# The last wait of a decode kernel, moved from SyncE's program to GpSimd's

## The chip, the cores and the metric

The kernel runs on one core of a Trainium2 chip. A core has five engines that each run a program of their own: TensorE (PE in the profile, its weight loads PEld), VectorE (DVE), ScalarE (ACT), GpSimd (POOL) and SyncE (SP). They meet only through semaphores: an instruction or a transfer adds to one, another instruction waits until it has a given value. SyncE computes nothing; here it issues nearly all transfers between the chip's main memory (HBM) and the on-chip buffer.

The metric is the device time of one execution in microseconds (us), as a median of several. It covers more than the instructions of the kernel: the span, from the first to the last recorded instruction of the program, is a little shorter than the measured time.

## The reference

One decode step for two sequences (one new token each, 512 features): attention over a cached context of 4096 positions with 32 heads of 128, a small two-layer network on the same two tokens, and a gate that mixes the two results.

```python
g = sigmoid((A_x * gate_w).sum(-1))
q = A_x @ A_wq                                      # 2 x (32 heads x 128)
p = softmax(q . A_k_cache * 128 ** -0.5)            # over 4096 positions, per head
a = (p . A_v_cache) @ A_wo                          # 4096 -> 512
b = relu(A_x @ B_w1) @ B_w2                         # 512 -> 1376 -> 512
out = g * a + (1 - g) * b                           # 2 x 512, bfloat16
```

Both halves read A_x. Keys and values are 64 MB each, so the 145 MB that are read set the scale of the work.

## The kernel before

The keys and the values (2 sequences x 32 heads x 4096 rows of 128) are cut into 8 units each, 32768 rows or 8 heads a unit. Three regions of the on-chip buffer take the units in turn, in the order written out in `order` (L185): five units of keys, then values and keys alternating, then the rest of the values. SyncE issues each unit's transfer as soon as TensorE is done with the unit that last used its region. VectorE transposes the keys, TensorE makes scores, ScalarE the exponentials, GpSimd spreads the probabilities into a masked layout, and TensorE multiplies them with the values. The last unit of values comes in two transfers (LASTV, L20).

After the last unit SyncE issues w2 (L252) and the output weights wo in four pieces (L255, WO_IN at L231), each with a semaphore of its own, wo0 to wo3. In the end TensorE runs `project` (L615): 32 steps of two products, each pair accumulating 2 x 512 results, the later steps waiting for the pieces of wo. When the last product is done, VectorE (L623) and ScalarE (L625) each convert one half of the result to bfloat16 and add 1 to the semaphore `cast`. SyncE waits for `cast` to be 2 and issues the output's transfer (L257), 2 KB, which adds 16 to the semaphore `out` when it has landed. Then SyncE waits for `out` to be 16 (L258, added by the call at L694).

All of this is written out by hand. Each helper (`sp`, `pool`, `dve`, `act`, `pe`) appends an operation to the list of one engine in `_Prog`; at the end `emit` (L77) writes the lists, each engine's operations in the order in which they were appended. An operation's waits become separate conditions ahead of it. So the order of calls at the bottom of the function is the order of each engine's program; only the relative order of calls for the same engine matters.

Three of the programs have operations in their ends that compute nothing: `fill` (L609) appends n increments of a semaphore that nobody waits for (L613). ScalarE gets five after its last copy ahead of the final half (L688) and five after it (L695), VectorE three and five (L689, L696), GpSimd three at once (L690) and four more that wait for the third piece of wo (L691). GpSimd's last real work is the spreading of the probabilities for the last unit of values; after that its program holds only these increments. TensorE's program ends with a branch that is never taken back (`never_back`, L634). Nothing in the kernel follows SyncE's wait for the output.

The lines around the change:

```python
    sp(lambda e: e.dma_start(out.rearrange("b s n -> (b s) n"), out_sb).then_inc(sem["out"], 16), dwaits=[(sem["cast"], 2)])
    tail_sp = [lambda: sp(lambda e: e.wait_ge(sem["out"], 16))]
...
    fill("pool", 3)
    fill("pool", 4, [(sem["wo2"], 16)])
    project()
    never_back()
    tail_sp[0]()
    fill("act", 5, [(sem["cast"], 2)])
    fill("dve", 5, [(sem["cast"], 2)])
```

Of the kernel before, what the change touches and what calls it, by code (L numbers as in the profile page):

```python
# [94 lines left out]
def bass_gated_mix__gqa_block_cached__dense_activation_relu__decode_kernel(  # L95
# [12 lines left out]
    P = _Prog(nc)  # L108
# [71 lines left out]
    sem = {n: nc.alloc_semaphore("sem_" + n) for n in names}  # L180
# [20 lines left out]
    def sp(fn, waits=(), dwaits=()):  # L201
        P.add("sp", fn, waits=waits, dwaits=dwaits)
# [52 lines left out]
        sp(lambda e, i=i, a=a, b=b: e.dma_start(wo_sb[:, a * 512:b * 512], A_wo.rearrange("(p r) n -> p (r n)", r=32)[:, a * 512:b * 512])  # L255
           .then_inc(sem[f"wo{i}"], 16))
    sp(lambda e: e.dma_start(out.rearrange("b s n -> (b s) n"), out_sb).then_inc(sem["out"], 16), dwaits=[(sem["cast"], 2)])  # L257
    tail_sp = [lambda: sp(lambda e: e.wait_ge(sem["out"], 16))]  # L258


    def constants():
# [347 lines left out]
    def fill(name, n, dwaits=()):  # L609
        if name not in P.fill:  # L610
            P.fill[name] = nc.alloc_semaphore("fill_" + name)
        for i in range(n):
            P.add(name, lambda e: e.sem_inc(P.fill[name], 1), dwaits=(dwaits if i == 0 else ()))  # L613
# [20 lines left out]
    def never_back():  # L634
        def fn(e):
            e.reg_mov(reg["p"], 1)
            e.br_lt(reg["p"], 1, on_true="rest", on_false="last").branch_hint(hint[0])
            enter("last", "main", engines=[mybir.EngineType.PE, mybir.EngineType.DVE, mybir.EngineType.Activation, mybir.EngineType.Pool,
                                   mybir.EngineType.SP])
        pe(fn)  # L640
# [50 lines left out]
    fill("pool", 4, [(sem["wo2"], 16)])  # L691
    project()
    never_back()
    tail_sp[0]()  # L694
    fill("act", 5, [(sem["cast"], 2)])  # L695
    fill("dve", 5, [(sem["cast"], 2)])  # L696

    P.resolve()

# [35 lines left out]
```

## Time and profile before

| | |
|---|---|
| measured time, median of 3 runs | 342.76 us (342.52 to 342.91) |
| the profiled execution: its own time | 342.64 us |
| the profiled execution: its span | 341.3 us |
| mean granted TensorE clock | 0.835 |
| read from HBM | 145.43 MB, 426 GB/s over the span |
| TensorE, VectorE, GpSimd, ScalarE busy | 209.9, 155.4, 41.8, 13.9 us |
| SyncE's issue of the output (L257) | starts at 340.13 us, takes 0.33 |
| SyncE's wait for the output (L258) | ends with the span, at 341.3 us |

A profile is one execution. Times in it count from the start of the span, and instructions are named by engine and by line of the kernel (L257 is line 257). An engine's name with a q (SPq, POOLq) stands for its sequencer, which waits, branches and issues transfers; that time is not counted as busy. A waiting instruction is recorded from the moment at which its wait is over, so its start tells when it was released. The view "chain that ended last" follows work back from the end; it starts at the last instruction that counts as work, so waits and transfers after that are not in it and have to be read from the timeline, from the view of an engine's waits and from single source lines.

Beside instructions, the trace records the time of each change of each semaphore, the landings of transfers included, and each packet that a transfer queue moved. These records go on for about 1.4 us after the last instruction of the kernel, up to 342.76 us.

### The profile page before, as it was taken

The numbers are of one execution on the slowest core, as the hardware profiler recorded it, in microseconds if no ns is written. First come the engines' busy times: TensorE is split into PE (matmuls) and PEld (weight loads), VectorE is DVE, ScalarE is ACT, GpSimd is POOL, SyncE is SP. The second block draws the span as 40 slices with busy tenths as digits, with TensorE's granted clock in tenths as the row PEclk, the third lists the DMA queues.
The fourth block names the chain that finished last, engine by engine and source line by source line (L and its number), as shares of the span: only waits on it lengthen the run. The fifth ranks groups of instructions, "written<-read, shape, count | busy, mean of one in ns | idle before, by whom it ended". The sixth has DMA issues, their size and how long they took to land. (4 is left out here: it accounts for less than half of the span.)

```text
span 341.3 us, 3101 instructions
## 1 busy us (share of the span) xinstructions
PE 209.9 (61%) x1243; PEld 33.9 (10%) x843; DVE 155.4 (46%) x45; ACT 13.9 (4%) x37; POOL 41.8 (12%) x53
## 2 busy tenths in 40 slices
PE   0080079685968909972995059820993773718387
PEld 0040011000100101110111001100100100101024
DVE  1010897979799769229800693019805000000111
ACT  2001000000000020000000000000003000000000
POOL 1000000000000004005002300050000235050400
PEclk9999999999898965996799559965696659676789
DMA  8998989898999999998989898989999999999896
GB/s 346 434 492 369 492 369 492 369 492 369 492 392 468 399 461 445 415 484 376 492 369 492 369 492 369 492 369 492 392 468 392 468 438 424 398 441 461 374 440 264
DMA packets 3580, 145.46 MB, mean 426 GB/s; under 512 B 405, under 2 KB 634, under 8 KB 762
## 3 DMA queue, kind: packets, MB, share of 16 engines
q1 hardware_dynamic: 3460, 145.33, 98.7%
q10 hardware_dynamic: 118, 0.10, 0.1%
q8 instruction: 1, 0.02, 0.0%
q14 instruction: 1, 0.01, 0.0%
HBM read 145.43 MB, written 0.00 MB: 426 GB/s over the span
## 5 line engine op out<-in xcount | busy, mean ns | idle before, releaser
L404 DVE STREAM_TRANSPOSE kv<-kv 128x8192 uint32<-128x8192 uint32 (+1 forms) x17 | 138.6, 8186 | 74.4 <-DMA kv<-in_A_k_cache_dram 74.4
L314 PE MATMUL PS<-kv,zero 128*128 (+1 forms) x544 | 130.3, 421 | 40.4 <-PEq L481 40.4
L314 PE MATMUL PS<-kv,ptw 128*32 x512 | 48.1, 469 | 11.7 <-issue 11.5
L320 PE MATMUL PS<-zero 32*128 32x512 bf16 (+2 forms) x21 | 9.7, 537 | 57.6 <-ACT zero L410 20.3
L449 POOL TENSOR_TENSOR ptw<-E,mask 128x512 bf16<-128x512 bf16 x32 | 32.2, 1038 | 21.1 <-PE PS L314 10.9
L467 DVE TENSOR_TENSOR X<-PS,maskc 128x512 f32<-128x512 f32 x2 | 1.4, 692 | 64.1 <-PE PS L314 64.1
L314 PEld LDWEIGHTS PS<-kv,zero 128*128 (+1 forms) x144 | 13.6, 103 | 154.6 <-issue 154.6
L393 POOL TENSOR_TENSOR zero<-q_sb,mask 128x32 bf16<-128x32 bf16 x8 | 1.9, 251 | 147.0 <-PE PS L314 123.3
L471 POOL TENSOR_TENSOR X<-X,maskc 128x512 f32<-128x512 f32 x6 | 6.2, 1039 | 109.2 <-ACT X L470 109.2
L314 PE MATMUL PS<-X,zero 128*64 128x512 f32 x16 | 11.6, 819 | 12.3 <-PEq L481 12.3
L314 PEld LDWEIGHTS PS<-kv,ptw 128*32 x512 | 8.7, 99 | 50.4 <-issue 49.7
L320 PEld LDWEIGHTS PS<-zero 32*128 32x128 bf16 x21 | 2.1, 109 | 69.4 <-issue 43.7
L373 DVE STREAM_TRANSPOSE ptw<-PS 128x1024 f32<-128x1024 f32 x1 | 1.3, 1251 | 16.4 <-PE PS L320 16.4
L415 DVE TENSOR_REDUCE zero<-PS 128x2 f32<-128x2048 f32 x2 | 4.5, 2271 | 9.1 <-PE PS L314 9.1
L470 ACT ACTIVATE X<-PS 128x512 f32<-128x512 f32 x6 | 3.6, 597 | 71.4 <-PE PS L314 71.4
L422 ACT ACTIVATE nrow<-mmax 128x32 f32<-128x32 f32 x2 | 0.5, 228 | 132.8 <-DVE mmax L419 132.8
L440 DVE STREAM_TRANSPOSE E<-E 128x2048 bf16<-128x2048 bf16 x2 | 4.6, 2300 | 2.4 <-ACT E L430 2.4
L410 ACT ACTIVATE zero<-zero 1x1 f32<-1x1 f32 x9 | 1.8, 200 | 84.9 <-DMA kv<-in_A_v_cache_dram 67.9
L430 ACT ACTIVATE E<-PS,negm 128x1024 bf16<-128x1024 f32 x4 | 4.4, 1109 | 0.6 <-DVE negm L426 0.6
L284 PE MATMUL PS<-kv 3*128 3x3 bf16 x4 | 0.3, 165 | 6.5 <-DMA kv<-in_gate_w_dram 6.5
L598 PE MATMUL PS<-kv,oW 128*2 128x256 bf16 x64 | 4.0, 272 | 0.4 <-DMA kv<-in_A_wo_dram 0.4
L314 PEld LDWEIGHTS PS<-X,zero 128*64 (+1 forms) x16 | 1.8, 161 | 15.8 <-issue 15.6
(49 smaller groups left out, 27.6 us busy)
## 6 DMA issues: line engine op xcount, KB each, us to landing
kv<-in_A_v_cache_dram SPq DMA_DIRECT2D x1, 6144.0 KB, 36.7
kv<-in_A_wq_dram SPq DMA_DIRECT2D x1, 4096.0 KB, 15.0
kv<-in_A_wo_dram SPq DMA_DIRECT2D x1, 2560.0 KB, 35.9
kv<-in_A_v_cache_dram SPq DMA_DIRECT2D x1, 2048.0 KB, 41.3
kv<-in_B_w_dram SPq DMA_DIRECT2D x1, 1376.0 KB, 5.8
kv<-in_B_w_dram SPq DMA_DIRECT2D x1, 1280.0 KB, 30.1
kv<-in_A_wo_dram SPq DMA_DIRECT2D x1, 1024.0 KB, 37.9
kv<-in_A_wo_dram SPq DMA_DIRECT2D x1, 384.0 KB, 38.4
```

The source lines that it names most:

```text
L314: return e.add_instruction(mybir.InstMatmult(name=nc.get_next_instruction_name(), engine=mybir.EngineType.PE, ins=[rhs, lhsT], outs=[e.low ...
L320: return e.matmul(dst, lhsT=nil, rhs=nil.unsqueeze(1).to_broadcast([32, 4, 128]) if n == 512 else nil[:, 0:n], start=not stop, stop=stop, ...
L393: pool(lambda g: g.tensor_tensor(out=out, in0=q, in1=msk, op=ALU.mult), waits=([["act_q", "dve_mask8"], []] + [[f"pesc_{x}"] for x in rang ...
L404: ins = v.transpose(out=reg[:, 4096 * p0:4096 * p1], in_=reg[:, 4096 * p0:4096 * p1])
L410: return lambda a: a.activation(out=tick[:, 2 + i:3 + i], in_=tick[:, 0:1], func=ACT.Copy).then_inc(sem["go"], n)
L415: dve(lambda v: v.tensor_reduce(out=mpad[:, 0:2], in_=PSF[:, 0:2048].rearrange("p (x h q) -> p h x q", h=2, q=16), axis=AX.XY, op=ALU.max) ...
L430: act(lambda a, h=h: a.activation(out=E[:].rearrange("p (x h q) -> p h x q", h=2, q=16)[:, h], in_=PSF[:, 0:2048].rearrange("p (x h q) -> ...
L440: dve(lambda v: v.transpose(out=E[:], in_=E[:]), waits=[f"act_exp{b}"], signal=f"dve_et{b}")
L449: pool(lambda g, src=src, dst=dst: g.tensor_tensor(out=dst, in0=src, in1=msk, op=ALU.mult), waits=(([f"dve_et{b}"] if ub == 0 else []) + ( ...
L470: act(lambda e: e.activation(out=X2[:], in_=src, func=ACT.Copy), waits=[f"pe_v_{v}"], signal=f"act_x_{v}")
L471: pool(lambda e: e.tensor_tensor(out=X, in0=X, in1=msk, op=ALU.mult).then_inc(sem["xg"], 1), waits=[f"act_x_{v}"] + ([] if v else ["dve_se ...
L598: pe(lambda e, g=g: e.matmul(psf(64 * g, 64 * g + 2, FIN_C0, 256), lhsT=w, rhs=m[:, 256 * g:256 * g + 256], start=start, stop=stop, tile_p ...
```

## The change

SyncE's wait for the output is removed, and the same wait is appended to GpSimd's list, after its increments. SyncE's program now ends with the issue of the output (L257). In the built program that is all: each engine has the same instructions in the same order, except that the wait for `out` stands as the last instruction of GpSimd instead of the last of SyncE.

```diff
     sp(lambda e: e.dma_start(out.rearrange("b s n -> (b s) n"), out_sb).then_inc(sem["out"], 16), dwaits=[(sem["cast"], 2)])
-    tail_sp = [lambda: sp(lambda e: e.wait_ge(sem["out"], 16))]
...
     project()
     never_back()
-    tail_sp[0]()
     fill("act", 5, [(sem["cast"], 2)])
     fill("dve", 5, [(sem["cast"], 2)])
+    P.add("pool", lambda e: e.wait_ge(sem["out"], 16))
```

## The prediction, made before the result was known

> **What bounds the kernel, and its end.** I read the page first, then the chain that ended last, then what SyncE waited for, then the timeline of the last microseconds, and at last the times at which semaphores changed. The page gives the span; over it the 16 DMA engines are busy in nearly every slice, so the body is a stream of transfers:
>
> ```profile
> span 341.3 us, 3101 instructions
> ...
> DMA  8998989898999999998989898989999999999896
> ...
> q1 hardware_dynamic: 3460, 145.33, 98.7%
> ```
>
> The change touches nothing of that stream. In the chain (start, duration, what) the stream ends with the last piece of wo, and a short tail follows:
>
> ```profile
> 300.10 37.89 DMA kv<-in_A_wo_dram
> 337.99 0.04 issue
> 338.03 1.64 PE PS L598 x24
> 339.67 0.02 issue
> 339.69 0.41 DVE ptw L623
> ```
>
> The tail goes on outside the chain, since waits and DMA issues are not counted as work. The timeline from 338 has the two casts and the issue of the output, and the view of SyncE's waits (waiter, what ended the wait, total us, times, longest) has the line that the change takes out of SyncE:
>
> ```profile
> 339.69 0.38 ACT L625 ACTIVATE ptw<-PS 2x256 bf16<-2x256 f32 x1 [5.21 <-PE PS L598]
> 339.69 0.41 DVE L623 CAST ptw<-PS 2x256 bf16<-2x256 f32 x1 [5.82 <-PE PS L598]
> 340.13 0.33 SPq L257 DMA_DIRECT2D out_dram<-ptw  x1
> ```
>
> ```profile
> SPq L258 <- DMA out_dram<-ptw: 0.8, 1, 0.8
> ```
>
> The views by source line place the waiting instruction and the increments that fill the ends of the other programs:
>
> ```profile
> L258 SPq EVENT_SEMAPHORE  x1: 17/17/17, 341.3 to 341.3; - x1
> ```
>
> ```profile
> L613 ACTq EVENT_SEMAPHORE  x10: 17/17/17, 334.3 to 340.7; - x10
> L613 DVEq EVENT_SEMAPHORE  x8: 21/21/21, 333.5 to 340.9; - x8
> L613 POOLq EVENT_SEMAPHORE  x7: 17/17/17, 315.8 to 339.6; - x7
> ```
>
> So SyncE's wait ends the span, at 341.329 us. GpSimd's program was over at 339.638, and the output is last in either kernel. What can differ is only what lies between the landing of the output and the end of the measured time: the profiled execution took 342.64 us, 1.31 more than its span. The trace shows that stretch through semaphores. Number 2 is named by no instruction of the kernel and changes nine times just after it, then nine times again (us from the span's start):
>
> ```
> first nine    340.003 340.938 340.976 341.175 341.446 | 341.489 341.527 341.561 341.608
> second nine   342.399 342.433 342.471 342.515 342.538 | 342.637 342.676 342.710 342.756
> ```
>
> I read each nine as a closing round in which five engines take turns up and then down. Steps in which nobody is late are 34, 38, 44 and 23 ns. Answers to ordinary semaphores, from the change waited for to the waiter's own change, cost ScalarE 45 ns (340.114 to 340.159), GpSimd 49 (339.003 to 339.052) and VectorE 57 (340.114 to 340.171): about 11 more than 34, 38 and 44, in the same order. So the second turn is ScalarE's, the third GpSimd's, the fourth VectorE's; the fifth, fastest and latest, is SyncE's, and the first TensorE's. The late turns fit: 340.938 follows ScalarE's last increment (340.722), 341.175 VectorE's (340.931), and 341.446 SyncE's wait (341.312).
>
> **The change, part by part.**
>
> *Removed: one wait at the end of SyncE.* Its program then ends with the issue, at 340.131 + 0.331 = 340.462 us, 0.87 earlier. With SyncE's own 0.134 from its last instruction's start to its turn, it would be ready near 340.6. By itself this uncovers VectorE: the fourth turn stays at 341.175 and the fifth would follow 0.023 later, 0.25 us before today's 341.446. Nothing stands behind the removed wait in SyncE's queue, and no transfer is issued there later.
>
> *Added: one wait at the end of GpSimd.* It is moved past GpSimd's seven increments (L613), which have no readers, and GpSimd issues no transfers; behind the wait stands only the closing round, and for that all five engines wait. The landing itself doesn't move: the casts, the issue and its packets stay as they are, with the last change of the output's semaphore at 341.296. The 0.25 us are thus never seen: GpSimd's turn, the third, now comes last.
>
> *The sum from the landing on.* Before: SyncE's wait starts 0.016 us after the landing and its turn is 0.134 later (341.446); from the fifth turn to the ninth 0.162 (341.608). That is 0.312 us.
> After: (a) GpSimd's answer: its L613 increment that waits for a landing started 0.024 after it (339.003 to 339.027). (b) From the start of its last instruction to its turn: the trace doesn't show it, since GpSimd had been done for long. Near rows: SyncE 0.134, ScalarE 0.216 (340.722 to 340.938), VectorE 0.244 (340.931 to 341.175). I take 0.23, between ScalarE and VectorE, as GpSimd's increments come every 0.08 us against 0.07 and 0.095 for those two. Ends: not below 0.025 (an increment's own time, 339.027 to 339.052); and not above 1.355, since GpSimd's third turn came at 340.976, right behind the second, counted from its last increment at 339.621. (c) From the third turn to the ninth with all others waiting: in the second nine 0.285 (342.471 to 342.756); in a round ahead of the kernel in which the third turn was the late one, 0.301. I take 0.293. It is more than four steps' 0.162 as two turns are added and as VectorE, just past its fourth turn, is not at once ready for its sixth (0.122 between them in the second nine).
> Sum: 0.024 + 0.23 + 0.293 = 0.547 us, against 0.312: **+0.235 us**. With the near rows' ends it is 0.443 to 0.569, so +0.13 to +0.26; with the far ends +0.02 to +1.37. All of these are losses, since the links after the landing grow in number whatever (b) is; a gain would have to come from outside this round (below).
>
> [...]
>
> **How it goes on the clock.** The profiled execution's 342.64 + 0.235 is 342.88 us. It lies 0.12 below the median of the three timed runs, 342.76 (342.52 to 342.91); on the median the change gives 342.995, **343.0 us**. That is +0.07%, inside the 0.2% that is about what a measurement of this kernel can tell from no change.
>
> **Rivals.**
>
> *Slower: GpSimd stalls on its way to the closing round.* There are gaps in the ends of three programs that no wait explains: between the last two increments (L613) of ScalarE from 340.360 to 340.722 (0.36 us), of VectorE from 340.448 to 340.931 (0.48), and in GpSimd from 339.123 to 339.537 (0.41). They stand close to the end of each program, hidden today behind the output. If one more instruction in GpSimd brings such a gap behind the wait, it adds 0.36 to 0.48, and the change costs +0.60 to +0.72; the far end of (b) gives +1.37, 344.1 us on the median. It decides from (b) = 0.69 on: above that the loss is over 0.2%. Against: GpSimd's gap lies before its last two increments, so the added instruction comes after it; and GpSimd idles some 1.7 us in the wait, time enough to have fetched what follows.
> [...]
>
> *Faster: SyncE's closing work sets the end.* After 341.329 the trace has two transfers of the instruction kind on queue 14, at 341.410 (0.53 us) and 341.620 (0.49, to 342.113). If they are SyncE's and the end waits for them, SyncE's earlier end starts them up to 0.87 earlier: 342.76 - 0.87 = 341.9 us, -0.25%. Against: the fifth turn of the second nine comes 0.023 after the fourth, so SyncE was not late there; TensorE, first in it at 342.399, was.
>
> *Nothing: the measured time doesn't hang on the round's end.* If it hung on the landing alone, the time would stay at 342.76. Against: 1.31 us of the measured time lie around the span, while the round's first part after it takes 0.28.
>
> **Chances.** Forecast (+0.02 to +0.55): 0.62. Slower rival (+0.55 to +1.4): 0.20, of which 0.17 beyond +0.69. Faster rival: 0.10, of which 0.08 beyond -0.69. Nothing: 0.08. So faster 0.08, same 0.75, slower 0.17. The range is 342.4 to 344.1 us: below, the lowest timed run less a tenth, as a time that stays may also fall there; above, the far end of (b) on the median. It leaves out the faster rival.
>
> **What would show it.** In the profile of the changed kernel the span should stay at 341.3 us, now ended by GpSimd's wait (start near 341.32, if the landing stays), SyncE's program should end near 340.46, and the time beyond the span should grow from 1.31 to about 1.55. In semaphore 2's first nine, the long pause should lie before the third change, some 0.25 us after the landing, with the last six in a row in about 0.29. A third change 0.7 us or more after the landing would be the slower rival. A time below 342.1, or second nine that do not shift with the first, would break the picture of the round. An output that lands at another distance from its issue (1.165 us now, 340.131 to 341.296) would be a cause I have priced at nothing.

## The result, and the profile after

The changed kernel takes 343.18 us (median of 18 runs, 343.05 to 343.55), the kernel before 342.64 us in its runs on the same chips (18 runs, 342.48 to 343.39). The ratio is 1.0015 with a 95% interval of 1.0008 to 1.0021: a loss of about 0.5 us. The interval lies above 1, so there is a loss, though at 0.15% it is under the 0.2% that the prediction took as what can be told from no change. The prediction had 343.0 us and +0.235 us: the direction and the way are right, but the forecast's size is under half of the +0.54 measured.

The page's span, and the chain from the last piece of wo on (start, duration, what), of the changed kernel:

```profile
span 341.6 us, 3101 instructions
```

```profile
299.43 38.89 DMA kv<-in_A_wo_dram
338.32 0.04 issue
338.37 1.60 PE PS L597 x24
339.97 0.02 issue
339.99 0.41 DVE ptw L622
```

The chain is the one of before, with about the same durations behind wo; all of it lies 0.30 us later. I take that for the spread between executions and not for an effect of the change: this one took 343.48 us, the second longest of the 18 (the 18 runs of the kernel before differ by 0.91 us among themselves), and the casts were over at 340.416 against 340.114 before, ahead of anything that the change touches. So I compare from the landing of the output on. The timeline has the issue of the output as SyncE's last line, the view of SyncE's waits (window from 290 us) has lost its line for the output, and the source line of the added wait shows when it ended:

```profile
340.43 0.33 SPq L257 DMA_DIRECT2D out_dram<-ptw  x1
```

```profile
SPq L257 <- DVE ptw L622: 39.6, 1, 39.6
SPq L252 <- PE PS L313: 13.8, 1, 13.8
```

```profile
L695 POOLq EVENT_SEMAPHORE  x1: 17/17/17, 341.6 to 341.6; - x1
```

The issue starts at 340.432 and the output lands at 341.598, 1.166 us later (1.165 before). GpSimd's wait ends the span, 0.041 us after the landing (0.033 before, by SyncE). What grew lies behind: the measured time is 1.841 us longer than the span in this execution, 1.311 before. It does so in every run: with the spans rounded to 0.1 us, the difference has a median of 1.84 us over 18 runs (1.81 to 1.88), and of 1.29 over 21 runs of the kernel before (1.26 to 1.35).

The changes of semaphore 2, from each kernel's own landing of the output (us):

```
before  first   -1.293 -0.358 -0.320 -0.121 0.150 | 0.193 0.231 0.265 0.312     second from 1.103
after   first   -1.292 -0.359  0.579  0.622 0.645 | 0.743 0.781 0.817 0.864     second from 1.652
```

The pause has moved from before the fifth change to before the third, as it should if the third turn is GpSimd's. The other numbers tell the size: 0.579 from the landing to that turn, where I had 0.254. From the ninth change to the measured end it is 1.03 us before and 1.02 after. "Measured end" stands here and below for the measured time counted from the start of the span. No record shows where the measurement itself begins and ends, and the last change of semaphore 2 comes 0.12 to 0.13 us behind that point; so what the argument rests on is that the distance stays the same, and not how long it is.

### The profile page after: what moved, and what is told of

It is laid out like the page before. It is cut to its first block, busy times and chain, and to the rows that moved or that the text cites. A ratio compares the mean times of both kernels' runs of the same rounds, so it can differ in the third digit from the quotient of the medians.

```text
span 341.6 us, 3101 instructions
## 1 busy us (share of the span) xinstructions
PE 209.6 (61%) x1243; PEld 33.8 (10%) x843; DVE 155.4 (45%) x45; ACT 13.9 (4%) x37; POOL 41.8 (12%) x53
## 5 line engine op out<-in xcount | busy, mean ns | idle before, releaser
L313 PEld LDWEIGHTS PS<-zero,kv 128*128 (+1 forms) x44 | 3.0, 158 | 3.5 <-issue 3.5
```

Of the source, the lines that this page charges most:

```text
L313: return e.add_instruction(mybir.InstMatmult(name=nc.get_next_instruction_name(), engine=mybir.EngineType.PE, ins=[rhs, lhsT], outs=[e.low ...
```

## The experiments

The theory: the measured end follows the ninth change at a fixed distance; the ninth change follows the turn of whichever engine is late; each engine has a stretch of its own between its last instruction and its turn; and GpSimd's is long, 0.555 us, against SyncE's 0.134. The rivals: a gap as in the ends of the programs that the added instruction brought behind the wait; a slow start after a release, whatever the engine; and a gain from SyncE's early end that is hidden under a larger loss. A version without any wait for the output, which would show what is next late, was not tried: its program could end before the output's semaphore had its last change.

**Four increments behind GpSimd's wait.**

```diff
     P.add("pool", lambda e: e.wait_ge(sem["out"], 16))
+    fill("pool", 4)
```

> As the changed kernel, with four more increments in GpSimd's program behind its wait for the output. The three theories of the 0.555 us between the start of that wait and GpSimd's turn in the closing round: (1) a long stretch of GpSimd's own at the end of any program: the increments come 0.08 apart, the last one's start to the turn is again 0.55, the wait's start to the turn 0.87, and the time beyond the span is that of the changed kernel, while the span grows by 0.33. (2) A gap like the 0.41 before GpSimd's last two increments, at a place counted in instructions from the program's start, now just behind the wait: it shows between two of the four increments, and the last one's start to the turn is 0.14 to 0.23. (3) Slow first steps after any release: the gap shows between the wait and the first increment, and the last one's start to the turn is about 0.23.

343.28 us in the profiled execution; the output lands at 341.128. GpSimd's increments by source line, the last of them ending the span at 341.4:

```profile
L612 POOLq EVENT_SEMAPHORE  x11: 17/17/17, 315.7 to 341.4; - x11
```

The wait merged into the first of the four, so they start at 341.152, 341.230, 341.308 and 341.387, without a gap. The third change is at 341.972: 0.585 from the last increment, 0.820 from the first. A gap among the instructions and a slow start after the release are both out; the long stretch lies behind all of the kernel's own instructions. The third change is 0.27 later after the landing than in the changed kernel, and so is the measured end (2.15 against 1.88).

**No increments in GpSimd's program.**

```diff
-    fill("pool", 3)
-    fill("pool", 4, [(sem["wo2"], 16)])
```

> As the changed kernel, without GpSimd's seven increments: its wait for the output follows its last real work directly, and the gap of 0.41 us that stood before the last two increments has no increments to stand between. (1) Long stretch of GpSimd's own: the wait's start to the turn is 0.555, plus 0.41 if the gap is a place in the program and now falls behind the wait, so 0.97, and the measured time is 343.6 us. (2) A gap that the added instruction brought behind the wait: with seven instructions fewer it falls elsewhere, and the stretch is 0.14 to 0.23 or again 0.55. (3) Slow release: 0.55.

343.18 us. The source line of GpSimd's wait:

```profile
L693 POOLq EVENT_SEMAPHORE  x1: 17/17/17, 341.3 to 341.3; - x1
```

The wait starts at 341.325 and the third change is at 341.880: 0.555 again, to the nanosecond. My 0.97 is wrong: the gap of 0.41 us, which in the profiles with these increments stands before the last two of the seven, doesn't show up in front of the turn. So the seven increments have no part in the 0.555.

The semaphore records show where the gap most likely went. Between the two nines most semaphores change once more, in five groups of about fifty numbers each. The group from 105 to 155 begins 0.057 to 0.060 us after the ninth change in the eleven other profiles and 0.414 after it here; the other four groups begin as in those profiles. GpSimd's is the only program that is shorter here, so I take this group for GpSimd's, and the 0.36 us for the gap, which lengthens the step from one increment to the next by about as much (0.431 against 0.079 in the kernel before): it sits at a place counted in GpSimd's instructions, and with seven fewer it lies behind the turn. There it costs nothing, as the second nine begins 0.778 us after the ninth change against 0.783 to 0.791 in the others.

**The wait in ScalarE's program, in VectorE's, in TensorE's.**

```diff
-    P.add("pool", lambda e: e.wait_ge(sem["out"], 16))
+    P.add("act", lambda e: e.wait_ge(sem["out"], 16))
```

and the same with "dve" and "pe".

> The wait for the output stands last in ScalarE's program instead of GpSimd's. Round theory (the end follows the waiting engine's turn, each engine with its own stretch): 0.02 from the landing to the wait, 0.22 to ScalarE's turn, the second, and 0.32 for the seven turns that follow it in an unbroken round: 0.56 from the landing to the ninth change against 0.31 with the wait in SyncE and 0.86 in GpSimd, so about 342.9 us. Rival (a program released by the output is slow to the round whatever the engine): 0.02 + 0.55 + 0.32 = 0.90, 343.2 us.

> The wait for the output stands last in VectorE's program. Round theory: 0.03 from the landing to the wait, 0.24 to VectorE's turn, the fourth, and 0.24 for the five that follow: 0.51 from the landing to the ninth change, about 342.85 us. Rival (slow release whatever the engine): 0.03 + 0.55 + 0.24 = 0.82, 343.15 us.

> The wait for the output stands last in TensorE's program, behind its branch. Round theory: TensorE has the first turn, so all nine follow the landing: 0.03 to the wait, a stretch of TensorE's own that is not known (0.13 as ScalarE's in the wait's form, up to 0.58, what its branch's start to its turn was before), and 0.357 for the unbroken round: 0.52 to 0.97 from the landing to the ninth change, so a measured time of 1.02 more than that after the landing (1.02 is the distance from the ninth change to the measured end in all six profiles so far). If the first turn is not TensorE's, the first change stays before the landing, and a later one moves.

342.63, 342.68 and 343.34 us in the profiled executions, which differ in when the output lands; so again from the landing on. The wait's line in each of the three:

```profile
L695 ACTq EVENT_SEMAPHORE  x1: 17/17/17, 341.1 to 341.1; - x1
```

```profile
L695 DVEq EVENT_SEMAPHORE  x1: 21/21/21, 341.3 to 341.3; - x1
```

```profile
L695 PEldq EVENT_SEMAPHORE  x1: 51/51/51, 341.7 to 341.7; - x1
```

With the two kernels of the study (us; the last column is the measured time less the landing):

```
wait in    landing  to wait  wait to turn  turn    to the ninth  sum    to the measured end
SyncE      341.296  0.016    0.134         fifth   0.162         0.312  1.344
VectorE    341.225  0.027    0.166         fourth  0.242         0.435  1.455
ScalarE    341.125  0.021    0.131         second  0.324         0.476  1.505
TensorE    341.696  0.028    0.238         first   0.359         0.625  1.644
GpSimd     341.598  0.024    0.555         third   0.285         0.864  1.882
```

In each it is the waiting engine's change that follows the landing, and the changes ahead of it stay before the landing. So the order of the turns is TensorE, ScalarE, GpSimd, VectorE, SyncE. The last column less the sum is 1.02 to 1.03 in all five. A slow start whatever the engine is out: ScalarE and VectorE are quicker to their turns than I had them (0.131 and 0.166 where I had 0.22 and 0.24 from their increments). SyncE has the shortest sum of the five.

**VectorE's wait, timed, and both waits.**

```diff
     P.add("pool", lambda e: e.wait_ge(sem["out"], 16))
+    P.add("sp", lambda e: e.wait_ge(sem["out"], 16))
```

> The wait in VectorE's program, timed. Its one profile had 0.435 us from the landing to the ninth change against 0.312 before and 0.864 in the changed kernel; so +0.12 us on the kernel before (342.76 on 342.64), which 0.2% can't tell from no change, and 0.43 less than the changed kernel's 343.18. A rival by which the time follows the number of turns behind the wait alone (six behind GpSimd's turn, five behind VectorE's, four behind SyncE's) has it midway between the two, +0.27.

> Both waits: SyncE's as before and GpSimd's as changed. Round theory: SyncE's turn, the fifth, is behind GpSimd's third, which comes 0.58 after the landing, so SyncE's wait costs nothing: 0.86 from the landing to the ninth change, 343.18 us, +0.15% on the kernel before, as the changed kernel. If removing SyncE's wait had gained something that GpSimd's wait then overspent, the time would be longer than 343.18 by that much.

With the wait in VectorE 342.63 us (11 runs), ratio 1.0004 (0.9995 to 1.0013); the kernel before had 342.55 in these rounds. That can't be told from no change by itself. The measured time less the span, which leaves out when the output lands, has a median of 1.41 us, 0.12 over before's 1.29, as the sums say (0.435 less 0.312); the rival's +0.27 is out. With both waits it is 343.14 us, ratio 1.0017 (1.0008 to 1.0027), and 1.84 beyond the span, as in the changed kernel. SyncE's wait is over at the same time as GpSimd's:

```profile
L695 POOLq EVENT_SEMAPHORE  x1: 17/17/17, 341.1 to 341.1; - x1
```

```profile
SPq L696 <- DMA out_dram<-ptw: 0.8, 1, 0.8
```

The first line is the source line of GpSimd's wait, the second that of SyncE in the view of its waits. From the landing to the ninth change it is 0.863 us against 0.864 in the changed kernel. So SyncE's wait costs nothing beside GpSimd's, and its removal gains nothing: no gain is hidden under the loss.

**A drain behind the wait.**

```diff
     P.add("pool", lambda e: e.wait_ge(sem["out"], 16))
+    P.add("pool", lambda e: e.drain())
+    fill("pool", 2)
```

> As the changed kernel, with a drain and two increments in GpSimd's program behind its wait for the output. What GpSimd does in the 0.555 us of its own is open; one candidate is a drain. If a drain of the idle engine is what takes long, the first increment comes 0.3 to 0.5 us after the wait, and the ones behind the drain start 0.08 apart. If a drain of the idle engine is short, the first increment comes 0.1 to 0.2 after the wait. In both cases the last increment's start to the turn is again 0.585, as with four increments, since that stretch lies behind all of the kernel's own instructions.

343.34 us. The wait and one of the increments merged into the drain:

```profile
L696 POOLq DRAIN  x1: 41/41/41, 341.3 to 341.3; - x1
```

It takes 0.041 us, and the increment left starts 0.106 after its start. A drain of the idle engine is short here and can't by itself make up the stretch. From that increment (341.443) to the third change (342.026) it is 0.583.

**GpSimd late without the output.** The last pair leaves SyncE's wait where it was and makes GpSimd's program longer, with increments that the casts release.

```diff
     fill("dve", 5, [(sem["cast"], 2)])
+    fill("pool", 16, [(sem["cast"], 2)])
```

and the same with 4.

> The kernel before, SyncE's wait in place, with four more increments at the end of GpSimd's program that are released by the casts, not by the output. If GpSimd's stretch to its turn is its own at any end (0.585 from the last increment's start), the last increment starts 0.27 us after the second cast and the turn is ready 0.85 after it, some 0.3 before the landing: hidden, 0.31 us from the landing to the ninth change, as before. If the long stretch belongs to a release by the output's landing, also hidden: the two agree here, and this run is the base of the next.

> The kernel before, SyncE's wait in place, with sixteen increments at the end of GpSimd's program that are released by the casts. The last one starts 0.02 + 15 x 0.08 = 1.2 us after the second cast, about when the output lands. If GpSimd's stretch is its own at any end, its turn comes 0.585 later, 0.6 us after the landing, the ninth change 0.285 after that: 0.9 us from the landing, and a measured time of 1.02 more, about 0.6 above the kernel before, without GpSimd waiting for the output. If the long stretch belongs to a release by the output's landing, GpSimd is ready 0.2 us or so after its last increment, 0.25 after the landing, and the ninth change comes 0.5 to 0.55 after the landing, +0.2 us.

With four, 342.56 us. GpSimd's increments by source line:

```profile
L613 POOLq EVENT_SEMAPHORE  x11: 17/17/17, 315.8 to 340.3; - x11
```

The last increment starts at 340.297, 0.92 before the landing, and from the landing to the ninth change it is 0.315, as in the kernel before (0.312). With sixteen, 343.18 us. Its views by source line have GpSimd's increments and SyncE's wait:

```profile
L613 POOLq EVENT_SEMAPHORE  x23: 17/17/17, 315.8 to 341.3; - x23
```

```profile
L258 SPq EVENT_SEMAPHORE  x1: 17/17/17, 341.3 to 341.3; - x1
```

Their last instructions start 0.016 us (SyncE) and 0.029 (GpSimd) after the landing, and it is GpSimd that counts: its last increment starts at 341.281, the third change is at 341.865, 0.584 later, and the ninth is 0.898 after the landing where the theory had 0.9. A stretch that belonged to the release by the output would have given 0.5 to 0.55. No instruction of GpSimd waits for the output here, and the loss is nearly that of the changed kernel all the same (0.898 against 0.864 from the landing to the ninth change).

## Why the prediction was right, and where it was not

**Where the end is.** The steps that say that nothing upstream moves held: the chain has the same pieces, the output takes 1.166 us from issue to landing against 1.165, SyncE's program ends with the issue. That the measured time follows the ninth change is shown by all twelve profiles: 1.01 to 1.03 us lie between the two, while the sum ahead of it runs from 0.31 to 1.13. The sums themselves repeat from profile to profile: 0.312 and 0.315 where SyncE is the last, 0.435 and 0.436 with the wait in VectorE, 0.863 to 0.865 in the three in which GpSimd's program ends with the wait alone. The reading of the turns, taken from the speeds at which engines answer a semaphore, is confirmed by moving the wait through all five engines.

**The sum.** (a), GpSimd's answer to the landing, is 0.024 as predicted. (c), from its turn to the ninth change, is 0.285 where I had 0.293; the 44 ns a hop that the Trainium skill ("Runtime: NRT & Kernel Launch", "The ~15µs preamble/postamble breakdown") gives for the barrier ahead of a kernel, and not for the one behind it, are near the mean of these six steps, 47.5 ns, though single steps run from 23 to 98. **The step that failed in size is (b)**, GpSimd's stretch from its last instruction to its turn: 0.555 us, where I took 0.23. That is +0.325 of the 0.317 by which the sum fell short (0.547 against 0.864), the rest is (c)'s -0.008. Of the change's 0.552 us, 0.421 come from (b), GpSimd's 0.555 for SyncE's 0.134, 0.123 from the two more turns, 0.008 from the slower answer.

So the mechanism held, and the time fell into the range; that it fell into the forecast's own band is partly luck. The band went from +0.02 to +0.55, the slower rival's began there, and the loss is +0.54 by the medians and +0.552 by the two sums, at the very border.

Why I took too little: I scaled the hidden stretch by the spacing of GpSimd's increments, which is between ScalarE's and VectorE's. The spacing says what one instruction costs, and the stretch behind the program is not a fixed number of such instructions: ScalarE's and VectorE's came out at 0.13 and 0.17 behind a wait, GpSimd's at 0.555, with all three spacings alike. The trace of before bounded it only at 1.355, and the forecast's place in that range was a guess by likeness. What GpSimd does in its stretch remains open. The runs show that it is there behind a wait, behind an increment and behind a drain (0.555, 0.583 to 0.585), whether or not the output is waited for, with or without the increments of before, and that a drain of the idle engine takes 0.041 us, 0.106 with the way to the next instruction.

**The rivals.** *Slower, by a gap:* in the changed kernel the 0.41 us did not come behind the wait; with four more instructions there was still none. My reason against it, that GpSimd idles long enough in the wait, was poor all the same: the profile of before has the gap two increments after an idle time of 19 us (319.87 to 339.03), so idling doesn't take it away. That such a gap can move behind the wait, as the rival had it, the run without increments shows, but there it fell behind the turn as well, where it cost nothing. The deciding point, 0.69, was not reached by 0.555. *Faster, by SyncE's closing work:* out by the run with both waits. *Nothing:* out by the fixed 1.02 us. The signs for which the prediction told to look were right in kind; the time beyond the span went to 1.84 instead of 1.55.

## What to carry to other kernels

In these twelve profiles the measured time ends at a fixed distance behind a round through all engines, and the last wait belongs where the engine's own stretch to its turn plus the turns behind it is shortest: here SyncE (0.31 us), then VectorE, ScalarE, TensorE, and GpSimd last (0.86). An engine whose program is over early costs nothing, however long its stretch is; by an estimate, GpSimd's last increment could start as late as 0.56 us before the output's landing unseen (0.585 for the stretch, less 0.027, the latest place of its turn after the landing: VectorE's second turn at 0.193, less the 0.122 between its two turns and the 0.044 of its answer). The runs bracket that point without testing it: 0.92 before the landing was unseen, 0.029 after it was not. And a stretch that a profile hides is to be bounded and then measured by making that engine the last one; a likeness to other engines is not a price.

## What the runs showed that I had not expected

GpSimd needs 0.555 us from its last wait to its turn, more than twice TensorE's 0.238 and four times SyncE's 0.134, although its increments come every 0.078 us, between ScalarE's 0.07 and VectorE's 0.095. And an engine released by a wait is a little quicker to its turn than after an increment: ScalarE 0.131 against 0.216, VectorE 0.166 against 0.244, GpSimd 0.555 against 0.585.
